# The first expert's tokens in two passes, its first weights from another queue: a delta-rule layer followed by a hash-routed mixture of experts

## The chip, the cores and the metric

The kernel runs on one core of a Trainium2 chip. The metric is the device time of one execution in microseconds (us). The kernel before takes 504.96 us (median of 3 runs, 503.61 to 505.69).

## The reference, cut to what matters

The first stage is a recurrence over 768 positions for 4 batches of 8 heads with 48 columns each. Its answers `y` become 3072 rows of 384 columns. The second stage sends each row to one of 8 experts, which a hash of the row's token picks, and writes the expert's answer to the row's place.

```python
k_n = k / (np.linalg.norm(k, axis=-1, keepdims=True) + 1e-06)
for t in range(S):                                   # S = 768
    kt, vt, bt = (k_n[:, :, t], v[:, :, t], beta[:, :, t, None])
    y[:, :, t] = np.einsum('bhd,bhde->bhe', q[:, :, t], state)
    v_old = np.einsum('bhde,bhd->bhe', state, kt)
    state = state + bt[:, :, :, None] * np.einsum('bhd,bhe->bhde', kt, vt - v_old)
x = y.transpose(0, 2, 1, 3).reshape(B * S, H * D)    # 3072 x 384
expert_idx = token_ids * np.int64(2654435761) % np.int64(E)   # E = 8
for e in range(E):
    mask = expert_idx == e
    h = np.maximum(x[mask] @ w1[e], 0.0)             # 384 x 1024
    out[mask] = h @ w2[e]                            # 1024 x 384
```

All data are float32. In these inputs the largest expert has 423 rows, of which 300 come from the first 17 chunks and 320 from the first 18.

## The kernel before, in words

**The recurrence** is worked in 24 chunks of 32 positions (`chunk`, c = 0 to 23). Four chunks are a group (g = 0 to 5). For each group `inverse` builds a triangular inverse on VectorE, column by column (L554, L558, L562), from the products of the keys `GK`, turns it into `TU` (L576), and `spread_t` lays it out as `Tz`: the group's first chunk by VectorE (L490), the other three by four DMAs of GpSimd (L497). A chunk is a chain between TensorE and ScalarE: ask the state for the keys (L593), scale by `Tz` (L632, `pair<-R,Tz`), copy to `W` (L651), update the state in PSUM (L661), copy the state back to SBUF (L716 on ScalarE; in the last chunks one half on VectorE, L714). The answers go through L632 and L686 to `x_sb`, and `store` scatters the chunk's rows to the DRAM tensor `x_scratch` in the order of the experts (GpSimd, L691). The rows of an expert therefore lie together, the earliest chunks first. `scale_v` (L504) prepares the values of the next chunk.

**What sets the order.** Each piece of work of this stage is a `task` with an engine, a duration and what it reads and writes. `order` lists them for all engines by a cost model, `boost` and `shy` (a task is held back that long). Each engine then works its own list strictly in that order, and an instruction that waits holds up all behind it on its engine. GpSimd's DMAs share eight semaphores in turn, so that a DMA can also wait for the eighth one before it.

**The first weights.** When the last inverse is done, its memory is free. There `load_w_parts` puts the first expert's `w1` (3 parts of 512 KB) and `w2` (4 parts of 384 KB), issued on SyncE behind the next stores.

**The experts** follow in falling order of their row counts, with fixed widths of 424, 424, 392, 392, 380, 380, 366 and 366 columns. `fetch` reads an expert's rows from `x_scratch` (four DMAs, L1084; those of the first expert from SyncE and ScalarE), `turn` transposes them on VectorE to `xT` (L1097), `gemm1` makes h (8 blocks of 3 products, each matmul of float32 being two instructions: 48 in all, L1115), which ScalarE and VectorE clear of negative values in turn (L1118, L1120) from three PSUM banks, and `turned` makes the answers (3 blocks of 8 products, 48 instructions, L1145), whose weights are every third column of `w2`. VectorE transposes them back (L1147), and GpSimd scatters them to the output (L1152). The last expert takes another path (L1128). The weights of expert e + 2 are loaded while expert e runs. Rows beyond the widths go through a loop at the end (L1197), which these inputs do not need.

Of the kernel before, what the change touches and what calls it, by code (L numbers as in the profile page):

```python
# [20 lines left out]
def kernel(  # L21
# [32 lines left out]
    NOV = (N - CAP + P - 1) // P  # L54
# [30 lines left out]
    def load_w_parts(e, pool):  # L85
        w1_sb = pool.tile([P, CO, F], F32, name="w1_sb")
        w2_sb = pool.tile([P, FO, DIN], F32, name="w2_sb")
        w1 = moe_w1[bass.ds(e, 1)].rearrange("o d f -> (o d) f")
        w2 = moe_w2[bass.ds(e, 1)].rearrange("o f d -> (o f) d")
        parts = [lambda i=i: nc.sync.dma_start(  # L90
            out=w1_sb[:, i], in_=w1.rearrange("(p co) f -> p co f", p=P)[:, i])
                 for i in range(CO)]
        parts += [lambda i=i: nc.sync.dma_start(
            out=w2_sb[:, i:i + 2],
            in_=w2[i * P:(i + 2) * P].rearrange("(o p) d -> p o d", p=P)) for i in range(0, FO, 2)]
        return (w1_sb, w2_sb), parts
# [15 lines left out]
    with ExitStack() as phase1:  # L112
# [34 lines left out]
        GKs = tiles(3, "GK", [P, C, GC, HU, 2])  # L147
# [360 lines left out]
        def inverse(g):  # L508
# [4 lines left out]
            def dve(ns, reads, writes, emit):  # L513
# [4 lines left out]
                U, zero[:, :, None].to_broadcast([P, C, C]), ACT.Copy), shy=24000 if g == 1 else 0, boost=-6e4 if g == 1 else 0)  # L518
# [9 lines left out]
                root, ssq, ACT.Sqrt, scale=0.25), boost=5e4)  # L528
# [51 lines left out]
        last_iv, stores = [0], set()  # L580
# [21 lines left out]
        def chunk(c):  # L602
# [96 lines left out]
            stores.add(len(tasks))  # L699
# [26 lines left out]
        def routing():  # L726
# [79 lines left out]
            own = new([P, 3, E])  # L806
            r_start, r_id, r_cnt = own[:, 0], own[:, 1], own[:, 2]
# [10 lines left out]
            for to, of in ((r_start, start), (r_id, iota_f[:, 0:E]), (r_cnt, cnt)):  # L818
# [4 lines left out]
                 lambda: nc.vector.tensor_copy(own_i, own[:, 0:2]))  # L823

            def tail():
                places, caps, room = new([P, NB_MAX]), new([P, E]), new([P, E])
                for e in range(E):
                    if e == 0 or WIDTHS[e] != WIDTHS[e - 1]:
                        dv("memset", caps[:, e:], float(WIDTHS[e]), **on)
                dv("tensor_scalar", out=places, in0=iota_f[:, 0:NB_MAX], scalar1=float(TB),  # L830
                   scalar2=low_f[:, 0:1], op0=ALU.mult, op1=ALU.add, **on)
                dv("tensor_tensor", room, r_cnt, caps, op=ALU.min, **on)
# [9 lines left out]
                thr, many = new([P, E, NOV]), new([P, E, NOV])  # L842
                dv("scalar_tensor_tensor", out=thr, in0=iota_f[:, None, 0:NOV].to_broadcast(
                    [P, E, NOV]), scalar=float(P), in1=caps[:, :, None].to_broadcast([P, E, NOV]),
                   op0=ALU.mult, op1=ALU.add, **on)
                dv("tensor_tensor", many, r_cnt[:, :, None].to_broadcast([P, E, NOV]), thr,
# [49 lines left out]
        def note():  # L896
# [93 lines left out]
            for c in range(NU):  # L990
# [7 lines left out]
                if c % GC == 2 and c + 2 < NU:  # L998
                    spread_t((c + 2) // GC)
# [256 lines left out]
```

## Time and profile before

| | us |
|---|---|
| median of 3 runs | 504.96 |
| the profiled execution | 505.14 |
| its span, first to last instruction | 503.5 |
| TensorE (PE) busy | 443.9 |
| VectorE (DVE) busy | 246.8 |
| ScalarE (ACT) busy | 165.4 |
| GpSimd (POOL) busy | 168.1 |

The span is what the trace covers; 1.64 us of the execution lie around it. The recurrence takes the first 228 us. The experts take the rest, and from 244 us to 494 us TensorE has no gap. A transfer is listed by the engine that issued it (SPq is SyncE's queue).

### The profile page before, as it was taken

Reading aid. Unit: us, or ns where it says so; the run is one execution under the profiler, and the core shown is the slowest. Engines: PE = TensorE matmul, PEld = TensorE weight load, DVE = VectorE, ACT = ScalarE, POOL = GpSimd, SP = SyncE. Lnnn points to the kernel's source line nnn. Section 1 sums busy time; section 2 is a strip of 40 time slices with the busy share of each in tenths; the row PEclk is TensorE's granted clock in tenths of the full one; section 3 lists DMA queues with packets and bytes.
Section 4 is the critical chain, followed back from the end, with each engine's and each line's share of the span. In section 5 each row is a group of like instructions: output and inputs, shape, how many; then the busy total and the mean of one; then the engine's idle time right before and its main releaser. Section 6 shows DMA issues by size and latency. Waiting matters only on the chain. (4 is left out here: it accounts for less than half of the span.)

```text
span 503.5 us, 15633 instructions
## 1 busy us (share of the span) xinstructions
PE 443.9 (88%) x6448; PEld 328.9 (65%) x6448; DVE 246.8 (49%) x882; ACT 165.4 (33%) x349; POOL 168.1 (33%) x224
## 2 busy tenths in 40 slices
PE   7796998879879697690999999999999999999993
PEld 4674877768768686580466566576676767767651
DVE  7799899999999989720212121121212212212100
ACT  4588778767676546440000100101001010010100
POOL 9752123132232312311000731715417063260721
PEclk8788799999989869976899999999999999999998
DMA  7965455466572622916973706409054190000000
GB/s 139 151 134 116 97 108 111 103 116 119 109 122 60 114 66 57 270 62 120 316 261 65 274 17 175 167 15 313 27 168 173 24 306 19 13 33 0 35 25 30
DMA packets 98248, 58.26 MB, mean 116 GB/s; under 512 B 84118, under 2 KB 92769, under 8 KB 97280
## 3 DMA queue, kind: packets, MB, share of 16 engines
q1 hardware_dynamic: 88832, 42.47, 34.3%
q0 software_dynamic: 7136, 14.12, 10.0%
q10 hardware_dynamic: 2208, 0.67, 0.8%
q8 instruction: 51, 0.84, 0.7%
q14 instruction: 21, 0.17, 0.1%
HBM read 44.51 MB, written 10.65 MB: 110 GB/s over the span
## 5 line engine op out<-in xcount | busy, mean ns | idle before, releaser
L1152 POOL DMA_INDIRECT out_dram<-o_sb,idx x90 | 88.3, 981 | 159.1 <-DVE o_sb L1147 133.8
L1115 PE MATMUL h_ps<-xT,w_sb 128*128 128x424 f32 (+3 forms) x384 | 129.2, 497 | 11.8 <-DMA xr<-x_scratch 11.8
L1115 PEld LDWEIGHTS h_ps<-xT,w_sb 128*128 128x128 f32 x384 | 73.8, 192 | 65.2 <-issue 27.9
L1145 PE MATMUL o_ps<-h_sb,w_sb 128*128 128x424 f32 (+3 forms) x336 | 112.3, 494 | 0.0
L1145 PEld LDWEIGHTS o_ps<-h_sb,w_sb 128*128 128x128 f32 x336 | 84.4, 251 | 27.1 <-issue 0.3
L1118 ACT ACTIVATE h_sb<-h_ps 128x424 f32<-128x424 f32 (+3 forms) x32 | 15.9, 496 | 233.2 <-PE h_ps L1115 233.2
L1120 DVE TENSOR_SCALAR h_sb<-h_ps 128x424 f32<-128x424 f32 (+3 forms) x32 | 18.1, 565 | 108.2 <-PE h_ps L1115 108.2
L691 POOL DMA_INDIRECT x_scratch<-x_sb,slot x24 | 25.3, 1052 | 115.5 <-ACT MT L480 45.4
L562 DVE TENSOR_TENSOR U<-U,tmp 128x30 f32<-128x30 f32 (+9 forms) x180 | 57.8, 321 | 0.0
L558 DVE TENSOR_TENSOR tmp<-U,Ni 128x30 f32<-128x30 f32 (+9 forms) x180 | 57.6, 320 | 0.1
L1147 DVE STREAM_TRANSPOSE o_sb<-o_ps 128x384 f32<-128x384 f32 (+2 forms) x21 | 15.5, 740 | 84.2 <-PE o_ps L1145 84.2
L593 PE MATMUL bank<-S,KQ 128*32 128x96 f32 x1472 | 40.4, 265 | 9.1 <-ACT S L716 6.1
L593 PEld LDWEIGHTS bank<-S,KQ 128*32 128x32 f32 x1472 | 34.3, 118 | 13.7 <-ACT S L716 8.0
L554 DVE SCALAR_TENSOR_TENSOR U<-U,Ni 128x1 f32<-128x1 f32 (+30 forms) x186 | 42.1, 226 | 0.2
L716 ACT ACTIVATE S<-psS 48x768 f32<-48x768 f32 x43 | 34.6, 805 | 18.0 <-PE psS L661 14.8
L661 PE MATMUL psS<-W,K 32*112 32x96 f32 x736 | 28.4, 285 | 7.6 <-ACT W L651 3.9
L632 PE MATMUL bank<-W,MT 64*64 64x48 f32 x768 | 31.0, 234 | 2.0 <-issue 1.5
L661 PEld LDWEIGHTS psS<-W,K 32*112 32x112 f32 x736 | 23.6, 188 | 10.9 <-ACT W L651 5.1
L632 PEld LDWEIGHTS bank<-W,MT 64*64 64x64 f32 x768 | 27.5, 148 | 4.9 <-issue 2.4
L497 POOL DMA_DIRECT2D Tz<-TU x24 | 17.5, 738 | 31.1 <-ACT S L901 14.5
L326 POOL DMA_DIRECT2D Q<-in_q_dram x40 | 23.0, 583 | 4.0 <-PE early L361 3.6
L480 ACT ACTIVATE MT<-GQ,kmask 128x256 f32<-128x256 f32 x48 | 21.8, 504 | 0.4 <-DVE GQ L442 0.4
(141 smaller groups left out, 441.3 us busy)
## 6 DMA issues: line engine op xcount, KB each, us to landing
w_sb<-in_moe_w_dram SPq DMA_DIRECT2D x14, 1536.0 KB, 9.9
V<-in_v_dram SPq DMA_DIRECT2D x96, 48.0 KB, 2.7
K<-in_k_dram SPq DMA_DIRECT2D x89, 48.0 KB, 3.1
Q<-in_q_dram SPq DMA_DIRECT2D x56, 48.0 KB, 3.1
xr<-x_scratch SPq DMA_DIRECT2D x16, 145.5 KB, 3.3
Tz<-TU POOLq DMA_DIRECT2D x24, 96.0 KB, 4.1
Q<-in_q_dram POOLq DMA_DIRECT2D x40, 48.0 KB, 3.7
w_sb<-in_moe_w_dram SPq DMA_DIRECT2D x3, 512.0 KB
```

The source lines that it names most:

```text
L326: eng].dma_start(out=dst[quarter(b)],
L554: nc.vector.scalar_tensor_tensor(out=U[:, n, 0:n], in0=U[:, j, 0:n], scalar=Ni[:, j, n:n + 1], in1=U[:, n, 0:n], op0=ALU.mult, op1=ALU.add)
L558: nc.vector.tensor_tensor(t, U[:, j:n, 0:n].to_broadcast([P, m, n]), Ni[:, j, n + 1:, None].to_broadcast([P, m, n]), op=ALU.mult)
L562: nc.vector.tensor_tensor(U[:, n + 1:, 0:n], U[:, n + 1:, 0:n], t, op=ALU.add)
L593: nc.tensor.matmul(res[quarter(b), u], lhsT=KQ[:, u, a, quarter(b)], rhs=S0[:, b, u].rearrange("p r d -> p (r d)"), start=(a == 1 and u == ...
L632: nc.tensor.matmul(to[rows, h], lhsT=lhsT(rows, h), rhs=rhs[rows, h], start=(first and h == 0), stop=True, skip_group_check=True, tile_pos ...
L661: nc.tensor.matmul(late["S"][0:DP + D, b, 2 * D * u:2 * D * u + 2 * D], lhsT=K4[quarter(b), u].rearrange("p r d -> p (r d)")[:, 0:DP + D], ...
L691: put = nc.gpsimd.indirect_dma_start(out=x_dram[:, :], out_offset=bass.IndirectOffsetOnAxis(ap=slot[:, c:c + 1], axis=0), in_=x_sb.rearran ...
L716: put = nc.scalar.activation(S1[half(r), :, :, r], new[half(r), :, :, r], ACT.Copy)
L1115: nc.tensor.matmul(h_ps[:, :width], lhsT=w1_sb[:, co, fo * P:(fo + 1) * P], rhs=xT[:, co, :width], start=(co == 0), stop=(co == CO - 1))
L1145: nc.tensor.matmul(os_ps[i][:, 0:width], lhsT=w2_sb[:, fo, i::CO], rhs=h_sb[:, fo, 0:width], start=(fo == 0), stop=(fo == FO - 1))
L1152: scat = nc.gpsimd.indirect_dma_start(out=out_q, out_offset=bass.IndirectOffsetOnAxis(ap=idx[e][:, k:k + 1], axis=0), in_=o_sb[:, k], in_o ...
```

## The change

1. **Two passes for the first expert.** As soon as the stores of the first 18 chunks are in DRAM, SyncE fetches the expert's first 288 rows (`fetch_first`) into the memory of `TU0`, and VectorE transposes them to `first["xT"]`. Behind the last chunk TensorE runs both products for these 288 columns, and then again for the other 136. The store of chunk 18 waits for that fetch.
2. **The first weights** are issued in seven parts by GpSimd, behind the stores of chunks 13, 14, 18, 19, 20, 21 and 21. `w1_first` takes the memory in which the key products `GK` lie, so that its parts can come before the last inverse is done. GpSimd loads the expert's number into a register for it. The fifth expert uses the same memory again.
3. **Bookkeeping.** The tables for overflowing rows get a ninth entry, for the case that the 288 rows are not all there in time; with these inputs they are, and the loop at the end stays empty.
4. **Order.** The clearing of `U` for a new inverse is held back by 8000 ns in all groups behind the first two and loses its rank, and the square root of the last inverse is held back by 1500 ns. VectorE's values for a chunk come a little earlier among the steps of the inverse.
5. `fetch(1)` and `weights(1)` stand ahead of the first pass, and the PSUM banks of the two products change places.

```diff
+    EARLY, ECH = 288, 18
+    EB = EARLY // TB
+    LATE = WIDTHS[0] - EARLY
+    w1_first = ctx.enter_context(tc.tile_pool(name="wk", bufs=1, side="right")).tile(
+        [P, CO, F], F32, name="w1_first")
...
-        GKs = tiles(3, "GK", [P, C, GC, HU, 2])
+        GKs = [w1_first[:, i].rearrange("p (j c u r) -> p j c u r", c=GC, u=HU, r=2)
+               for i in range(3)]
...
             task("ACT", 951, (), (f"U{i}",), lambda: nc.scalar.activation(
-                U, zero[:, :, None].to_broadcast([P, C, C]), ACT.Copy), shy=24000 if g == 1 else 0, boost=-6e4 if g == 1 else 0)
+                U, zero[:, :, None].to_broadcast([P, C, C]), ACT.Copy), shy=24000 if g == 1 else 8000 if g else 0, boost=-6e4 if g else 0)
...
-                root, ssq, ACT.Sqrt, scale=0.25), boost=5e4)
+                root, ssq, ACT.Sqrt, scale=0.25), boost=5e4, shy=1500 if g == NG - 1 else 0)
...
-            task("POOL", 1150, (f"x{c % 2}", "slot", "number"), (f"x_dram{c}",), store, kb=200)
+            task("POOL", 1150, (f"x{c % 2}", "slot", "number") + (("first_x",) if c >= ECH else ()),
+                 (f"x_dram{c}",), store, kb=200)
+
+        def fetch_first():
+            first["x"] = TUs[0].rearrange("p x i -> p (x i)")[:, 0:EB * QW].rearrange(
+                "p (k y) -> p k y", y=QW)
+            rows = x_dram[bass.ds(regs[0][0], EARLY)].rearrange(
+                "(k t) (q y) -> q t k y", t=TB, q=QN)
+            for qt in range(QN):
+                nc.sync.dma_start(out=first["x"][TB * qt:TB * qt + TB, :, 0:DQ + 1],
+                                  in_=rows[qt][:, :, 0:DQ + 1])
+
+        def first_parts(c):
+            for n, at in enumerate(PARTS):
+                if at == c:
+                    names = ([f"GK{n}{cc}{r}" for cc in range(GC) for r in range(2)]
+                             if n < CO else [f"w2{n}"])
+                    reads = (f"x_dram{c}", "e0") + (() if n < CO else (f"TU{(NG - 1) % 2}",))
+                    task("POOL", 900, reads, names, lambda n=n: w_parts(regs[3], first.get(
+                        "w2"))[n](nc.gpsimd), kb=512 if n < CO else 384)
+
+        PARTS = (13, 14, 18, 19, 20, 21, 21)
...
-                    w_tiles[0], parts = load_w_parts(regs[1][0], w_pool)
-                if i in stores and parts:
-                    for part in parts[:3]:
-                        part()
-                    parts = parts[3:]
+                    first["w2"] = w_pool.tile([P, FO, DIN], F32, name="w2_first")
+                    first["h"] = w_pool.tile([P, FO, EARLY], F32, name="h_first")
+                    first["xT"] = w_pool.tile([P, CO, EARLY], F32, name="xT_first")
...
             fetch(0, [(nc.sync, regs[0][0]), (nc.scalar, regs[2])])
             for t in os_ps:
                 nc.vector.memset(t[:, min(WIDTHS):], 0.0)
+            fetch(1)
+            weights(1)
+            w1_sb, w2_sb = w_tiles[0]
+            gemm1(w1_sb, first["xT"], first["h"], EARLY)
+            o_sb = m_o.tile([P, NB_MAX, DQ], F32, name="o_sb")
+            for i in range(CO):
+                turned(w2_sb, first["h"], o_sb, i, EARLY, 0)
+            scatter(idx_first, o_sb, range(EB))
...
-                gemm1(w1_sb, xTs.pop(e), h_sb, WIDTHS[e], between)
+                width = WIDTHS[e] if e else LATE
+                gemm1(w1_sb, xTs.pop(e), h_sb, width, between)
```

**Where instructions move.** On ScalarE, at chunk 15, the square root of the last inverse (`root`) stood ahead of both copies of the state, before:

```order
L623 ACTIVATE R_103<-bank_158 128x192 x2
L651 ACTIVATE W_105<-pair 128x192 x2
L527 ACTIVATE root_153<-ssq_151 128x32
L716 ACTIVATE S_96<-psS 48x16x48 x2
L686 ACTIVATE x_sb_107<-bank_159 128x4x96
```

and now:

```order
L632 ACTIVATE R_111<-bank_163 128x192 x2
L660 ACTIVATE W_113<-pair 128x192 x2
L748 ACTIVATE S_104<-psS 48x16x48
L536 ACTIVATE root_158<-ssq_156 128x32
L748 ACTIVATE S_104<-psS 48x16x48
L695 ACTIVATE x_sb_115<-bank_164 128x4x96
```

It moved behind the first of the two copies; the second still stands behind it.

On GpSimd, chunks 17 to 19 before (`x_scratch<-x_sb` is a chunk's store, `Tz` the layout of the last inverse for chunks 21 to 23):

```order
L690 COPY x_sb_107<-number 128x4
L691 DMA x_scratch<-x_sb_107,slot 3520x400
L690 COPY x_sb_106<-number 128x4
L691 DMA x_scratch<-x_sb_106,slot 3520x400
L497 DMA Tz_135<-TU_137 32x24x32 x4
L690 COPY x_sb_107<-number 128x4
L691 DMA x_scratch<-x_sb_107,slot 3520x400
```

and now:

```order
L699 COPY x_sb_115<-number 128x4
L700 DMA x_scratch<-x_sb_115,slot 3520x400
L699 COPY x_sb_114<-number 128x4
L700 DMA x_scratch<-x_sb_114,slot 3520x400
L506 DMA Tz_140<-TU_142 32x24x32 x4
L699 COPY x_sb_115<-number 128x4
L700 DMA x_scratch<-x_sb_115,slot 3520x400
L99 ISA
L99 DMA w_first<-in_moe_w_dram 128x1024
```

Stores and layout keep their order. The second store shown, that of chunk 18, now waits for the early fetch, and the layout stands behind it; a part of the weights follows the store of chunk 19.

On ScalarE, at the end of the recurrence, before:

```order
L686 ACTIVATE x_sb_107<-bank_159 128x4x96
L1084 ISA
L1084 DMA xr<-x_scratch 32x14x97
L1084 ISA
L1084 DMA xr<-x_scratch 32x14x97
L1169 TENSOR_LOAD ov_i
L1118 ACTIVATE h_sb<-h_ps_4900 128x424
```

and now:

```order
L695 ACTIVATE x_sb_115<-bank_164 128x4x96
L1147 ISA
L1147 DMA xr<-x_scratch 32x5x97
L1147 ISA
L1147 DMA xr<-x_scratch 32x5x97
L1183 ACTIVATE h_first<-h_ps_4939 128x288
L1183 ACTIVATE h_first<-h_ps_4941 128x288
```

ScalarE's two fetches of the remaining rows, which wait for the last store, still stand first; its share of the first pass stands behind them.

## Rows read from the trace of the kernel before

**Rows 1.** Windows of 40 us: length, busy time (and count) by engine, granted clock, DMA.

```profile
160.00:200.00 40.00, 32.57 (x960) 29.03 (x949) 36.88 (x147) 22.37 (x52) 10.24 (x15) 0.83 0.36 78
```

**Rows 2.** Timeline, end of the recurrence: start, length, what, idle before it and releaser.

```profile
227.15 1.14 PE L632 MATMUL bank<-W,MT 64*64 64x48 f32 x32 [0.49 <-ACT W L651]
228.39 0.49 ACT L686 ACTIVATE x_sb<-bank 128x384 f32<-128x384 f32 x1 [1.06 <-issue]
229.65 0.98 POOL L691 DMA_INDIRECT x_scratch<-x_sb,slot  x1 [3.12 <-issue]
232.65 3.55 SPq L1084 DMA_DIRECT2D xr<-x_scratch  x6
232.92 1.22 ACTq L1084 DMA_DIRECT2D xr<-x_scratch  x2
239.07 2.10 DVE L1097 STREAM_TRANSPOSE xT<-xr 128x448 f32<-128x448 f32 x3 [6.43 <-DMA xr<-x_scratch]
240.06 19.25 PE L1115 MATMUL h_ps<-xT,w_sb 128*128 128x424 f32 x48 [11.77 <-DMA xr<-x_scratch]
```

**Rows 3.** Timeline of TensorE alone, three stretches of equal matmuls, start and length.

```profile
276.22 6.21 PE L1115 MATMUL h_ps<-xT,w_sb 128*128 128x424 f32 x17
...
451.77 10.62 PE L1145 MATMUL o_ps<-h_sb,w_sb 128*128 128x366 f32 x34
...
101.62 0.60 PE L361 MATMUL pair<-ident,Q 128*128 128x128 f32 x4
```

**Rows 4.** Groups by line, TensorE's weight loads: count, busy us, mean ns, idle before.

```profile
L1145 PEld LDWEIGHTS o_ps<-h_sb,w_sb 128*128 128x128 f32 x336 | 84.4, 251 | 27.1 <-issue 0.3
L1115 PEld LDWEIGHTS h_ps<-xT,w_sb 128*128 128x128 f32 x384 | 73.8, 192 | 65.2 <-issue 27.9 <-DVE xT L1097 0.4 <-DVE o_sb L1147 0.2
L593 PEld LDWEIGHTS bank<-S,KQ 128*32 128x32 f32 x1472 | 34.3, 118 | 13.7 <-ACT S L716 8.0 <-issue 4.8 <-ACT x_sb L686 0.6
```

**Rows 5.** Timeline around two waits of ScalarE, chunks 6 and 15.

```profile
108.79 1.06 ACT L517 ACTIVATE U<-zero 128x1024 f32<-128x1024 f32 x1 [2.43 <-DVE TU L576]
...
171.72 0.23 ACT L527 ACTIVATE root<-ssq 128x32 f32<-128x32 f32 x1 [2.92 <-DVE ssq L524]
...
173.52 2.79 PE L593 MATMUL bank<-S,KQ 128*32 128x96 f32 x64 [2.78 <-ACT S L716]
```

**Rows 6.** Windows of 4 us, columns as in rows 1.

```profile
172.00:176.00 4.00, 2.48 (x64) 2.44 (x64) 3.86 (x21) 3.28 (x7) 1.41 (x4) 0.53 0.73 124
...
212.00:216.00 4.00, 3.52 (x78) 3.23 (x76) 0.74 (x1) 1.24 (x3) 0.19 (x1) 0.65 0.89 324
242.00:246.00 4.00, 4.00 (x10) 1.96 (x9) 0.00 (x0) 0.53 (x1) 0.00 (x0) 0.76 0.95 388
```

**Rows 7.** Timeline, chunks 17 to 21.

```profile
184.48 0.57 DVE L504 TENSOR_TENSOR bank<-V,ntok 128x384 f32<-128x384 f32 x1 [1.84 <-ACT R L623]
...
191.15 0.98 POOL L691 DMA_INDIRECT x_scratch<-x_sb,slot  x1 [6.07 <-ACT MT L480]
...
197.98 1.95 DVE L576 STREAM_TRANSPOSE TU<-U 128x1024 f32<-128x1024 f32 x1
...
200.55 2.94 POOL L497 DMA_DIRECT2D Tz<-TU  x4 [2.40 <-PE psS L661]
...
203.45 1.13 PE L632 MATMUL pair<-R,Tz 64*64 64x48 f32 x32
...
211.15 0.57 PE L593 MATMUL bank<-S,KQ 128*32 128x96 f32 x17 [2.67 <-issue]
...
211.66 1.24 PE L632 MATMUL pair<-R,Tz 64*64 64x48 f32 x32
```

**Rows 8.** DMA issues: whole run, then 180 to 235 us; KB each, median us to landing.

```profile
Tz<-TU POOLq DMA_DIRECT2D x24, 96.0 KB, 4.1
...
w_sb<-in_moe_w_dram SPq DMA_DIRECT2D x4, 384.0 KB, 12.2
Tz<-TU POOLq DMA_DIRECT2D x4, 96.0 KB, 7.5
```

More of the change, by code (lines that the diff above doesn't have):

```diff
@@ L578, in inverse @@
             last_iv[0] = len(tasks) - 1
-        last_iv, stores = [0], set()
+        last_iv, first = [0], {}
         def pairs(us):
@@ L697, in store, with turn_first @@
                 tc.add_to_no_dep_group("rows", put.ins)
-            stores.add(len(tasks))
-            task("POOL", 1150, (f"x{c % 2}", "slot", "number"), (f"x_dram{c}",), store, kb=200)
+            task("POOL", 1150, (f"x{c % 2}", "slot", "number") + (("first_x",) if c >= ECH else ()),
[8 more added lines that the diff above has]
+                                  in_=rows[qt][:, :, 0:DQ + 1])
+        def turn_first(i):
+            nc.vector.transpose(
+                first["xT"][:, i].rearrange("p (k t) -> p k t", t=TB), first["x"][:, :, i:DQ:CO])
+        def first_parts(c):
[7 more added lines that the diff above has]
+        PARTS = (13, 14, 18, 19, 20, 21, 21)
         to_load = {w: iter(range(AHEAD + 1, NU)) for w in "kq"}
@@ L999, in note, with first_e @@
                     spread_t((c + 2) // GC)
+                first_parts(c)
+                if c == ECH - 1:
+                    task("SP", 2000, tuple(f"x_dram{n}" for n in range(ECH)) + ("regs",),
+                         ("first_x", "TU0"), fetch_first, kb=450)
+                    for i in range(CO):
+                        task("DVE", 370, ("first_x", f"TU{(NG - 1) % 2}"), (f"xT{i}",),
+                             lambda i=i: turn_first(i))
                 if c == NU // 2:
                     registers_later[0]()
+                    def first_e():
+                        regs[3] = nc.values_load(own_i[0:1, 1, 0:1], min_val=0, max_val=E - 1,
+                                                 engines=[mybir.EngineType.Pool])
+                    task("POOL", 900, ("own", f"R{c % 2}0"), ("e0",), first_e)
                 if c == NU - 2:
@@ L1037 @@
             seq, start = order()
-            parts = []
             for i in seq:
@@ L1146, in turned, with scatter @@
                                  rhs=h_sb[:, fo, 0:width], start=(fo == 0), stop=(fo == FO - 1))
[L1147 removed]
+            nc.vector.transpose(o_sb[:, k0:k0 + n, i::CO],
                                 os_ps[i][:, 0:n * TB].rearrange("p (k t) -> p k t", t=TB))
[L1150 to L1151 removed]
+        def scatter(of, o_sb, blocks):
+            for k in blocks:
                 scat = nc.gpsimd.indirect_dma_start(
[L1153 to L1154 removed]
+                    out=out_q, out_offset=bass.IndirectOffsetOnAxis(ap=of[:, k:k + 1], axis=0),
                     in_=o_sb[:, k], in_offset=None, bounds_check=QN * N - 1, oob_is_err=False)
@@ L1172 @@
             places(0)
-            fetch(1)
-            weights(1)
             for e in range(E):
-                w1_sb, w2_sb = w_tiles.pop(e)
+                w1_sb, w2_sb = w_tiles[e]
                 def between(fo):
@@ L1190 @@
                             places(e + 1)
-                        turned(e, w2_sb, h_sb, o_sb, i)
-                    scatter(e, o_sb)
+                        turned(w2_sb, h_sb, o_sb, i, width, skip)
+                    scatter(idx[e], o_sb, range(skip, NBS[e]))
                 else:
```

120 lines of the change are left out of this document (74 added, 46 removed).

## Prediction

> **What bounds the kernel now.** I read the windows first, then the timeline around the end of the recurrence, then the waits of TensorE there, then TensorE's weight loads and the DMA issues. Two places matter.
>
> *The seam.* The last answers leave TensorE at 227.15 + 1.14 = 228.29. From there a single chain runs: answers to SBUF, the store at 229.65, its landing (SyncE can issue the fetch at 232.65, 3.0 later), the fetch and its flight, VectorE's transposes at 239.07, the first product at 240.06, with TensorE idle for 11.77 [rows 2]. The product then takes 19.25 for 48 instructions, because the granted clock is 0.76 in 242:246 and lower before [rows 2, 6]. Expert 1 begins at 276.22 [rows 3]. So the first expert occupies 276.22 − 228.29 = 47.93 us behind the recurrence. From 244 to 494 TensorE has no gap, so what starts earlier here ends earlier: the 227.3 us of rest of the span do not change.
>
> *The last inverse.* In 160:200 VectorE is busy for 36.88 of 40 [rows 1], with the inverse's columns; `TU` is ready at 197.98 + 1.95 = 199.93, and chunk 20 scales with it at 203.45. GpSimd issues the layout for the later chunks at 200.55, over 2.94, and chunk 21 scales only at 211.66 [rows 7]. Of these 8.2 us 2.67 are TensorE idle with "issue" as its reason [rows 7]; without them a chunk takes 5.5. At that time the first expert's weights are in flight: the layout's four DMAs land in 7.5, against 4.1 over the whole run, and the `w2` parts in 12.2 [rows 8]. I read the issue wait as instructions that came late through the same crowd; the trace shows only that both stand together.
>
> **How long a narrow pass takes.** Three stretches of equal matmuls fit one line, 0.84 ns a column plus 0.16 for the last one's drain: 17 × 424 columns give 6.05 + 0.16 = 6.21 (6.21 in the trace), 34 × 366 give 10.45 + 0.16 = 10.61 (10.62), 4 × 128 give 0.43 + 0.16 = 0.59 (0.60) [rows 3]. Nothing is added per instruction, though each has a weight load of its own: the loads lie beside the matmuls. So 288 columns are 0.242 each, 11.6 for 48. For 136 columns the matmul is 0.114, shorter than the mean load: 0.192 for the first product, 0.251 for the second, whose weights are every third column [rows 4]. A listed load may contain waiting, since 32 columns are listed with 0.118 [rows 4], and that is no quarter of 0.192. Lower ends for the 136 columns are 48 × 0.114 = 5.5 for each product; upper ends are 48 × 0.192 = 9.2 and 48 × 0.251 = 12.05. For contiguous weights I take 5.5, because the transposes with 128 contiguous columns and a load each do run at 0.11 [rows 3]. For strided ones no row is near; I take 0.17 (the listed 0.251 less the 0.08 that a load seems to have whatever its width, an estimate from 0.118 and 0.192), 8.2.
>
> The Trainium skill speaks against this change: "TensorE: Matmul & The Clock Gate", Part 3, says that a weight load overlaps running matmuls only when it targets other rows of the array, while Part 2 there also allows a load into a background buffer. By the first, a full-height load would add to every matmul; by the second it is hidden. The trace agrees with the second (0.84 ns a column at three widths, no constant). It stays a rival below.
>
> **Part 1, the two passes (term A).** The first pass waits for the last answers only; its fetch, transposes and weights are long done. Its chain:
> - start behind the last matmul: 0.1.
> - first product, 288 columns: 11.6, and in it a stall. ScalarE's own list has the two fetches of the late rows ahead of its evictions. They wait for the last store, and are issued up to 232.92 + 1.22 = 234.14 [rows 2]. TensorE can fill three PSUM banks, 18 matmuls or 4.35 us, to 232.7; the fourth block needs ScalarE's first eviction, done near 234.6. Stall 1.9. Bounds: 0, if the DMA issues don't hold ScalarE up, to 3.9, if the clock then falls and costs 2.0 as it did now (19.25 against 48 × 0.356 + 0.16 = 17.25).
> - second product, 288 columns: 11.6 (12.05 by the strided loads).
> - between the passes VectorE must transpose the last answers and then the late rows: 2.10 for 3 × 448 columns [rows 2] is 0.70 for one, hence 0.45 + 3 × 0.25 + 0.1 for semaphores = 1.3. The rows themselves have landed long before (239 against about 253). Bounds 0.5 to 2.
> - 136 columns: 5.5 and 8.2.
>
> Sum: 0.1 + 11.6 + 1.9 + 11.6 + 1.3 + 5.5 + 8.2 = 40.2, against 47.93: **A = −7.7**. With loads at full length 48.2, +0.3 (+2.3 with the clock's loss); with no stall and all loads hidden 35.6, −12.3.
>
> **Parts 2 and 4, the recurrence's end (term B).**
> - `root` waited 2.92 for VectorE and so kept back the state's copies: TensorE idled 2.78 at 173.52, and was granted 0.53 in 172:176, nearly all at 1.2 GHz [rows 5, 6]. VectorE in turn idled 1.84 at 184.48 for ScalarE [rows 7]. One copy now stands ahead of `root`, the other still behind, so half of the chain's delay may stay. Since VectorE sets when `TU` comes, only its gap counts: I take 1.5, bounds 0 and 3.1 (all that rows 1 leave idle).
> - The clearing of `U` waited 2.43 at 108.79 [rows 5]; that is early, and what it delayed was caught up before the inverse. Zero, bound −1.
> - The weights go out over chunks 13 to 21 and no longer in one burst. Layout at its usual 4.1: it is there 0.62 + 2.94 + 4.1 = 7.7 behind `TU`, not 11.7. Chunk 21 then follows chunk 20 by 5.5, and the 2.67 go (0 if the three last parts still crowd). Of 212:216, granted 0.65 [rows 6], some 70% ran at 1.2 GHz, which cost 1.4; I count them as gone, since the idle time before them is.
> - The parts cost GpSimd some 1 us each (0.7 for an issue, by 2.94 for four), beside 10.24 busy of 40 [rows 1]: hidden. What they could hide no more is late stores, which nobody waits for until the end.
> - The store of chunk 18 waits for the early fetch, and the layout stands behind it on GpSimd. Chunk 17's store at 191.15 [rows 7] + 3.0 landing + 6.4 (232.65 to 239.07 [rows 2]) = 200.55, when the layout is issued now: 0, since `TU` would be only 1.5 earlier. Bound: the fetch takes 12.2 as `w2` did, the layout goes out at 207.3, chunk 21 scales at 207.3 + 2.94 + 4.1 = 214.4, 2.7 later than now.
> - VectorE gets three transposes of 288 columns, 0.45 each, among the last chunks; two may delay a state copy: +0.9 (0 to 1.4).
>
> Sum: −1.5 − 2.67 − 1.4 + 0.9 = **B = −4.7**, bounds +3.6 and −8.6.
>
> **Parts 3 and 5** move a few loads and register reads to engines that wait: zero, ±0.5. 320 of the expert's rows come from 18 chunks, so all 288 are there and the loop stays empty.
>
> Total: 505.14 − 7.7 − 4.7 = 492.7. The profiled execution is 0.2 above the median, so **492.5 us**; its own range 488 to 497.
>
> **Rivals.**
> 1. *Weight loads set the pace of the 136 columns* with their full length (0.192, 0.251). For it: they are listed so [rows 4]. Against: 0.11 for transposes [rows 3]. A is +0.3: 505 without B, 500 with it. Chance 0.13.
> 2. *The recurrence gains in full, and strided loads are hidden*: `TU` 3.1 earlier, 2.67, both stretches of low clock gone (2.8), no cost on VectorE, second product 5.5: 505 − 8.6 − 7.7 − 2.7 = 486. For it: each loss has one cause in the rows. Against: VectorE has hardly a gap to give [rows 1]. Chance 0.17.
> 3. *The early fetch holds GpSimd*, so the layout comes later: B = +2.7, and 505.1 − 7.7 + 2.7 = 500. For it: both use one queue [rows 7]. Against: the crowd is gone. Chance 0.07.
> 4. *Slower: loads are not hidden in narrow passes but add.* The place is both products of 136 columns, 48 × (0.192 + 0.114) + 48 × (0.251 + 0.114) = 32.2 instead of 13.7, and A becomes +10.8: 516 without B, 511 with it. It decides from 0.08 us added per instruction (7.7 / 96). Against: no constant in rows 3. Chance 0.05.
>
> The forecast has 0.58. A run of this kernel can tell 0.5%, 2.5 us, from no change. Faster: forecast, rival 2, rival 3 and half of rival 1, 0.88; same 0.07; slower 0.05. The range, 484.5 to 501, leaves out rival 4, the bad half of rival 1 and a tail of rival 2.
>
> **What would show it.** Right: TensorE's first product directly behind the last answers; a wait for ScalarE at its fourth block; 136-column matmuls 0.114 apart in the first product and 0.15 to 0.2 in the second; layout landing in some 4 us; chunk 21 scaling 5 to 6 behind chunk 20; expert 1 at about 264. Wrong: spacing near 0.19 and 0.25 (rival 1) or 0.3 (rival 4); layout issued far behind `TU` (rival 3); clock still near 0.5 around chunks 15 and 21, or an end of the recurrence at 228 as now, which takes B away and leaves 497.

## The result, and the profile after

The changed kernel takes 499.62 us (median of 20 runs, 493.5 to 504.6), the kernel before 505.05 in 20 runs beside them (500.87 to 509.47). The ratio is 0.988, with a 95% interval of 0.985 to 0.991: faster by some 6 us, a little under half of the 12.5 forecast. The ratio leaves out executions more than 1.5% above the fastest of their kernel, seven of the changed kernel's 20, the traced one among them, and so comes out lower than the medians' 0.989. The time lies in the range, the size of the gain was missed.

The traced execution took 502.01 us, 2.4 above its median, with a span of 500.4. TensorE's timeline at the seam (start, length, what, idle before it and its releaser), which answers to [rows 2, 3]:

```profile
224.79 0.92 PE L641 MATMUL bank<-W,MT 64*64 64x48 f32 x25
226.35 4.63 PE L1180 MATMUL h_ps<-xT_first,w_first 128*128 128x288 f32 x18 [0.64 <-ACT x_sb L695]
231.72 7.54 PE L1180 MATMUL h_ps<-xT_first,w_first 128*128 128x288 f32 x30 [0.74 <-ACT h_first L1183]
239.10 11.80 PE L1210 MATMUL o_ps<-h_first,w_first 128*128 128x288 f32 x48
252.25 5.18 PE L1180 MATMUL h_ps<-xT,w_first 128*128 128x136 f32 x42 [1.34 <-issue]
258.48 0.96 PE L1180 MATMUL h_ps<-xT,w_first 128*128 128x136 f32 x6 [1.05 <-issue]
259.28 2.24 PE L1210 MATMUL o_ps<-h_sb,w_first 128*128 128x136 f32 x12
263.47 0.62 PE L1210 MATMUL o_ps<-h_sb,w_first 128*128 128x136 f32 x2 [1.95 <-issue]
264.97 6.95 PE L1210 MATMUL o_ps<-h_sb,w_first 128*128 128x136 f32 x34 [0.88 <-DVE h_sb L1185]
...
271.75 17.24 PE L1180 MATMUL h_ps<-xT,w_sb 128*128 128x424 f32 x48
```

The first pass is much as forecast: it starts 0.64 behind the last answers (0.1 forecast), waits 0.74 for ScalarE at its fourth block (1.9 forecast), and ends at 250.9; the gap to the second pass, the bubble below, is 1.35. Then the second pass takes 271.75 − 252.25 = 19.5 us where 13.7 were forecast. The first product's instructions are listed 0.12 apart, as forecast, but stop at the eighth block, and the second product's stop later for `h_sb`. The first expert comes to 46.0 us, against 47.93 before.

The other engines in the second pass. ScalarE and VectorE clear a block by turns as soon as it is complete (an eviction below), and so free its PSUM bank:

```profile
251.79 1.02 POOL L1217 DMA_INDIRECT out_dram<-o_sb,idx_first  x1 [23.64 <-DVE last_i L1243]
...
255.38 0.30 DVE L1185 TENSOR_SCALAR h_sb<-h_ps 128x136 f32<-128x136 f32 x1 [1.02 <-PE h_ps L1180]
...
258.14 0.28 ACT L1183 ACTIVATE h_sb<-h_ps 128x136 f32<-128x136 f32 x1 [3.18 <-issue]
...
260.30 0.30 DVE L1185 TENSOR_SCALAR h_sb<-h_ps 128x136 f32<-128x136 f32 x1 [4.63 <-PE h_ps L1180]
...
262.10 0.98 POOL L1217 DMA_INDIRECT out_dram<-o_sb,idx_first  x1 [0.30 <-issue]
...
263.13 0.28 ACT L1183 ACTIVATE h_sb<-h_ps 128x136 f32<-128x136 f32 x1 [4.71 <-remote]
...
264.62 0.30 DVE L1185 TENSOR_SCALAR h_sb<-h_ps 128x136 f32<-128x136 f32 x1 [4.01 <-PE o_ps L1210]
```

Four blocks are cleared 0.2 us behind their last matmul; the fifth to eighth come 2.3, 3.7, 5.9 and 5.3 us behind it (worked out from the starts and the spacing). Over the same stretch GpSimd runs the nine scatters of the first pass's answers, 1.28 us apart.

The last product ends 10.1 us before the span does (500.4 − 490.31):

```profile
474.67 15.64 PE L1193 MATMUL o_ps<-w_sb,h_sb 128*122 128x384 f32 x48
```

In the trace before it was 8.7 us (503.5 − 494.78):

```profile
479.14 15.64 PE L1128 MATMUL o_ps<-w_sb,h_sb 128*122 128x384 f32 x48
```

The prediction had nothing for this end.

### The profile page after: what moved, and what is told of

It is laid out like the page before. It is cut to its first block, busy times and chain, and to the rows that moved or that the text cites. A ratio compares the mean times of both kernels' runs of the same rounds, so it can differ in the third digit from the quotient of the medians.

```text
span 500.4 us, 15902 instructions
## 1 busy us (share of the span) xinstructions
PE 448.2 (90%) x6544; PEld 341.6 (68%) x6544; DVE 251.8 (50%) x903; ACT 165.2 (33%) x353; POOL 174.5 (35%) x231
## 5 line engine op out<-in xcount | busy, mean ns | idle before, releaser
L1217 POOL DMA_INDIRECT out_dram<-o_sb,idx x81 | 79.3, 979 | 133.0 <-DVE o_sb L1212 110.4
L1180 PE MATMUL h_ps<-xT,w_sb 128*128 128x392 f32 (+3 forms) x288 | 94.5, 488 | 0.0
L1183 ACT ACTIVATE h_sb<-h_ps 128x392 f32<-128x392 f32 (+4 forms) x32 | 14.9, 466 | 220.3 <-PE h_ps L1180 198.9
L1180 PEld LDWEIGHTS h_ps<-xT,w_sb 128*128 128x128 f32 x288 | 54.7, 190 | 38.2 <-issue 7.8
L1210 PE MATMUL o_ps<-h_sb,w_sb 128*128 128x392 f32 (+3 forms) x240 | 79.6, 491 | 0.0
L1210 PEld LDWEIGHTS o_ps<-h_sb,w_sb 128*128 128x128 f32 x240 | 60.3, 251 | 18.8 <-issue 0.2
L1185 DVE TENSOR_SCALAR h_sb<-h_ps 128x392 f32<-128x392 f32 (+4 forms) x32 | 16.9, 527 | 104.7 <-PE h_ps L1180 63.7
L1212 DVE STREAM_TRANSPOSE o_sb<-o_ps 128x384 f32<-128x384 f32 (+4 forms) x24 | 16.1, 671 | 84.2 <-PE o_ps L1210 84.2
L602 PEld LDWEIGHTS bank<-S,KQ 128*32 128x32 f32 x1472 | 34.0, 117 | 13.5 <-ACT S L748 7.4
L748 ACT ACTIVATE S<-psS 48x768 f32<-48x768 f32 x43 | 34.6, 806 | 19.7 <-PE psS L670 17.2
L1210 PE MATMUL o_ps<-h_sb,w_first 128*128 128x136 f32 (+1 forms) x96 | 25.3, 426 | 2.8 <-issue 1.9
L506 POOL DMA_DIRECT2D Tz<-TU x24 | 17.5, 738 | 24.1 <-ACT Tz L949 12.2
L1210 PEld LDWEIGHTS o_ps<-h_sb,w_first 128*128 128x128 f32 x96 | 21.4, 267 | 6.5 <-issue 2.1
```

The lines of the kernel that those rows point to most:

```text
L506: lambda b=b, x0=x0: nc.gpsimd.dma_start(out=Tz[quarter(b), x0:, b % 2], in_=TU[quarter(b), x0:]), kb=150)
L602: nc.tensor.matmul(res[quarter(b), u], lhsT=KQ[:, u, a, quarter(b)], rhs=S0[:, b, u].rearrange("p r d -> p (r d)"), start=(a == 1 and u == ...
L748: put = nc.scalar.activation(S1[half(r), :, :, r], new[half(r), :, :, r], ACT.Copy)
L1180: nc.tensor.matmul(h_ps[:, :width], lhsT=w1_sb[:, co, fo * P:(fo + 1) * P], rhs=xT[:, co, :width], start=(co == 0), stop=(co == CO - 1))
L1210: nc.tensor.matmul(os_ps[i][:, 0:width], lhsT=w2_sb[:, fo, i::CO], rhs=h_sb[:, fo, 0:width], start=(fo == 0), stop=(fo == FO - 1))
L1217: scat = nc.gpsimd.indirect_dma_start(out=out_q, out_offset=bass.IndirectOffsetOnAxis(ap=of[:, k:k + 1], axis=0), in_=o_sb[:, k], in_offse ...
```

## The experiments

Three pieces are read from each trace. B is the end of the recurrence, counted from the moment at which the first inverse's `TU` is ready, since the start-up before it varies by 4 us between executions. "First expert" runs from the last answers to expert 1. "End" is what follows the last product. The median is of all executions, the pieces are of one traced execution, which can lie up to 3.3 us beside it (`wait_sp` 496.27, `burst` 493.7). Three runs of one execution each (`noscat`, `four`, `drop`) stand in the text alone. `contig` takes other weights for 136 rows, `drop` leaves 288 rows unwritten.

| run, chip | median us | ratio to before | B | first expert (second pass) | end |
|---|---|---|---|---|---|
| before, first trace | 505.05 | | 182.3 | 47.9 | 8.7 |
| before2, 3 | 505.24 | | 181.4 | 49.2 | 8.7 |
| changed, first trace | 499.62 | 0.988 [0.985, 0.991] | 179.4 | 46.0 (19.5) | 10.1 |
| again, 7 | 499.54 | 0.990 [0.985, 0.995] | 177.4 | 46.1 (19.5) | 10.4 |
| early, 7 | 498.59 | 0.988 [0.983, 0.993] | 177.2 | 46.1 (19.5) | 10.0 |
| late, 7 | 501.06 | 0.993 [0.989, 0.997] | 178.8 | 46.1 (19.5) | 10.1 |
| contig, 7 | 498.9 | 0.985 [0.977, 0.993] | 179.7 | 45.3 (18.8) | 10.2 |
| even, 7 | 492.45 | 0.975 [0.970, 0.981] | 176.3 | 39.6 (17.1) | 10.1 |
| again2, 3 | 499.54 | 0.988 [0.984, 0.993] | 176.6 | 46.2 (19.7) | 10.2 |
| wait2, 3 | 491.67 | 0.973 [0.970, 0.976] | 177.8 | 40.6 (14.1) | 10.1 |
| even2, 3 | 494.02 | 0.976 [0.972, 0.980] | 178.6 | 39.6 (17.2) | 10.1 |
| wait, 5 | 489.08 | 0.973 [0.968, 0.978] | 173.4 | 41.3 (14.1) | 10.3 |
| burst, 5 | 490.88 | 0.976 [0.971, 0.982] | 175.6 | 41.0 (14.1) | 10.1 |
| order4, 5 | 492.37 | 0.980 [0.975, 0.986] | 175.4 | 40.8 (14.1) | 10.4 |
| again3, 1 | 490.72 | 0.976 [0.970, 0.983] | 174.7 | 41.3 (14.1) | 10.0 |
| wait_even, 1 | 489.39 | 0.972 [0.969, 0.976] | 176.4 | 39.0 (16.6) | 10.3 |
| wait_sp, 1 | 493.0 | 0.979 [0.975, 0.983] | 180.1 | 41.0 (14.1) | 9.3 |

**again.** No edit.

> The changed kernel once more, for a second trace. In its first trace the pieces of the sum came out as: end of the recurrence 2.6 us earlier (4.7 forecast), first expert 1.9 shorter (7.7 forecast), of which the second pass alone is 19.5 instead of 13.7. If these are features of the kernel, this trace shows the second pass at 19 to 20 again, with evictions that come 2 to 6 us behind their matmuls from its fifth block on. If they were an accident of one execution, the second pass takes 14 to 16 here.

The second pass took 19.5 us again, with evictions up to 4.6 us late. It is no accident of one execution. The recurrence ended 2.4 us earlier than in the first trace.

**early, late.** The third expert's weights are moved away from the second pass:

```diff
             weights(1)
+            weights(2)                 # early
...
-                        weights(e + 2)
+                        if e:
+                            weights(e + 2)
```

```diff
-                        weights(e + 2)
+                        for n in () if e == 0 else (2, 3) if e == 1 else (e + 2,):
+                            weights(n)     # late
```

> The third expert's weights (3 MB) are issued behind the second's, before the first pass, and so are in long before the second pass. Theory 1 (crowd: while the DMA engines are full, the signals between TensorE and the evicting engines come late, and narrow blocks have no slack for it): no late eviction in the second pass, 48 x 0.12 + 48 x 0.20 = 15.5 us instead of 19.5, time 4 us below the changed kernel, 495.5. Theory 2 (TensorE itself falls behind in narrow matmuls, since their weight loads take 0.19 to 0.25): second pass stays at 19 to 20, time within 1 us of the changed kernel. Theory 3 (GpSimd's nine scatters disturb): as theory 2.

> The third expert's weights are issued one expert later, behind the rows of the fourth. Theory 1 (crowd): second pass at 15 to 16 us instead of 19.5, time 4 us below the changed kernel, the same as with the early issue. Theory 2 (weight loads) and theory 3 (scatters): second pass stays at 19 to 20. If the late rows' small packets alone make the crowd, the second pass lies between, 17 to 18.

Both 19.5, with evictions as late as before, in `early` from the sixth block on with the DMA engines busy for a fifth of the time or less (254 to 260 us; for the fifth they were full). Theory 1, the crowd, falls for these blocks.

**contig.** Neighbouring columns of `w2` for the second product of the second pass:

```diff
-                nc.tensor.matmul(os_ps[i][:, 0:width], lhsT=w2_sb[:, fo, i::CO],
+                nc.tensor.matmul(os_ps[i][:, 0:width], lhsT=w2_sb[:, fo, i * P:(i + 1) * P] if k0 else w2_sb[:, fo, i::CO],
```

> In the second pass alone the second product takes its weights from 128 neighbouring columns of w2 instead of every third (so the answers of those 136 rows are not the reference's). If the strided load sets the spacing of 0.20 us there, the 34 unhindered matmuls come at 0.114 to 0.12 each, and the pass is some 4 us shorter in its unhindered part. If reading the rows or the clock sets it, it stays at 0.20. If the late signals alone rule the pass (theory 1), its end moves by less than 2 us.

The instructions now came 0.12 apart (median of the listed starts; 0.176 in `again`), so the stride does set that spacing. The pass shortened by only 0.75 us, and its last 34 instructions, behind the halts, took 6.26 us in place of 6.98. The clock explains the rest. Columns as in rows 1, first `contig`, then `again`:

```profile
261.00:267.00 6.00, 3.98 (x17) 3.98 (x18) 2.01 (x4) 0.00 (x0) 0.97 (x3) 0.50 0.82 305
...
261.00:267.00 6.00, 4.46 (x21) 4.47 (x22) 2.28 (x5) 0.00 (x0) 0.44 (x2) 0.72 0.69 256
```

At the lower clock (1.2 GHz) the instructions come 0.227 apart in both, so that the stride costs nothing there.

**four.** Every accumulation of the second pass four times:

```diff
-                for co in range(CO):
+                for co in list(range(CO)) * times:
...
-            for fo in range(FO):
+            for fo in list(range(FO)) * (4 if k0 else 1):
...
+                gemm1(w1_sb, xTs.pop(e), h_sb, width, between, 1 if e else 4)
```

> In the second pass every accumulation is run four times over into the same bank (results unchanged): 192 instructions of 136 columns in each product in place of 48. It measures the sustained spacing by itself. Theory 2, weight loads set it: 0.19 an instruction in the first product, so 27 us more there, 0.20 to 0.25 in the second, 29 to 36 more. If narrow matmuls are sustained at their listed spacing and only something at the pass's start is late: 0.116, 17 us more in the first, and 0.12 to 0.18 (17 to 26) in the second.

TensorE's timeline in that pass:

```profile
251.54 7.95 PE L1180 MATMUL h_ps<-xT,w_first 128*128 128x136 f32 x66 [1.35 <-issue]
...
262.54 0.51 PE L1180 MATMUL h_ps<-xT,w_first 128*128 128x136 f32 x3 [0.71 <-issue]
...
263.99 13.47 PE L1180 MATMUL h_ps<-xT,w_first 128*128 128x136 f32 x114 [0.43 <-issue]
277.30 22.90 PE L1210 MATMUL o_ps<-h_sb,w_first 128*128 128x136 f32 x131
```

The run took 540.66 us. 114 instructions of 136 columns run at 13.47 / 114 = 0.118 us, each with its own load of 128 columns; 131 with strided loads at 22.90 / 131 = 0.175. TensorE halts only between about 8 and 12 us behind the pass's start, in steps, with "issue" as the reason and inside a block of 24 instructions (66 is no multiple of it), so for no eviction; the second block's eviction comes 6.8 us late. Theory 2, that weight loads hold TensorE at 0.19 and more, falls. The Trainium skill says in "TensorE: Matmul & The Clock Gate", Part 3, that a weight load overlaps running matmuls only when it goes to other rows of the array. That does not show here either: 0.118 is 136 × 0.84 ns plus 0.004.

**noscat.** The scatters moved down GpSimd's list, behind the second pass:

```diff
-            scatter(idx_first, o_sb, range(EB))
...
+                    if e == 0:
+                        scatter(idx_first, o_sb, range(EB))
```

> The nine scatters of the first pass's answers are issued behind the second pass instead of beside it. Late evictions did not go away without the crowd of the weights (in the runs with earlier and later weights the second pass stayed at 19.5 us). Theory 3 (the scatters disturb): second pass 15 to 16 us here, no late evictions. Theory 2 (TensorE itself sustains no more in narrow matmuls, and the listed starts run ahead of it): 19.5 again.

It took 502.32 us, the second pass 19.7. Nothing was tested: nothing ahead of the scatters on GpSimd waits, so they went out at the same time as ever. A place in an engine's list delays nothing unless something ahead of it waits.

**even.**

```diff
-    EARLY, ECH = 288, 18
+    EARLY, ECH = 224, 18
```

> 224 early columns and 200 late ones instead of 288 and 136. Theory 2 (no matmul below 0.19 to 0.2 us, whatever its width): first pass 96 x 0.19 to 0.2 + 0.7, second 96 x 0.2, with the bubble of 1.5 some 40 to 41 us in place of 46.1, so 5 us less time than the changed kernel: 494. If width alone counted (0.84 ns a column) and a disturbance in the second pass adds 5.8 us to it: 18.8 + 1.5 + 16.1 + 5.8 = 42, 4 less. If nothing but the sum of the columns counts, 46, no change.

First expert 39.6 us. The evictions of the second pass are late here too, but by 3.3 us at most; they hold TensorE for 0.3 us at its eighth block, and the last of them starts 9.7 us behind the start of the pass. With seven scatters instead of nine that is 2.6 us sooner than in `again` (12.4), two scatters of 1.28. That pointed at GpSimd.

**drop, wait, burst, order4** ran together on chip 5.

```diff
-            scatter(idx_first, o_sb, range(EB))       # drop: only this
...
+                    if e == 0:                         # wait: these too
+                        nc.vector.tensor_copy(idx_late, idx_first)
+                        scatter(idx_late, o_sb, range(EB))
```

```diff
-        PARTS = (13, 14, 18, 19, 20, 21, 21)
+        PARTS = (19,) * 7                              # burst
```

```diff
-   ... shy=24000 if g == 1 else 8000 if g else 0, boost=-6e4 if g else 0)
+   ... shy=24000 if g == 1 else 0, boost=-6e4 if g == 1 else 0)      # order4
-                root, ssq, ACT.Sqrt, scale=0.25), boost=5e4, shy=1500 if g == NG - 1 else 0)
+                root, ssq, ACT.Sqrt, scale=0.25), boost=5e4)
```

> The nine scatters of the first pass's answers are left out (288 rows of the output stay unwritten). In the run that only moved them down GpSimd's list they still went out beside the second pass, since nothing ahead of them waits, so that run told nothing of them. Theory 3 (GpSimd's scatters hold back TensorE's signals as long as they run, some 12.3 us from the start of the second pass with nine, 9.5 us with seven): signals in time, second pass 48 x 0.118 + 48 x 0.175 + 0.2 = 14.3 us instead of 19.5. Theory 2 (a narrow stream holds itself back in its first 12 us): 19.5 as before.

> The same nine scatters are made to wait for the second pass's last transpose (they take their row numbers from a copy that VectorE makes there). Theory 3: second pass 14.3 us, first expert 40.8 instead of 46.1, time 5 us below the changed kernel, unless the scatters, now beside the second expert's wide product, cost there. Theory 2: no change from the changed kernel.

> All seven parts of the first weights are issued at once behind the store of chunk 19, nearly as before the change, the rest as in the changed kernel. If spreading them is worth what was forecast (2.7 of waiting at chunk 21 and up to 1.4 of low clock), the recurrence ends 3 to 4 us later than with pieces, at 227 to 228 for a last inverse at 198, and the layout of the last inverse lands late, 7 us instead of 4. If the queue by which they go out matters and not the crowd, it ends as in the changed kernel, 24 to 26 us behind chunk 19's answers.

> The clearing of U and the square root of the last inverse get their former delays and ranks back, the rest as in the changed kernel. If these orders bring VectorE's last inverse forward by 1.5 us as forecast, it is ready at 199.5 to 200 here instead of 198.1 (mean of eight traces), chunk 15 to 16 takes 8 to 9 us instead of 6.4, and the kernel is 1.5 us slower. If they bring nothing, 198 again.

All four have a second pass of 14.1 (`drop` took 490.83 us), `burst` and `order4` with their scatters beside it. So these alone did not make the late evictions. `burst` told against the forecast on another point: the recurrence ended 22.9 us behind the last `TU`, near the other runs of that chip (23.1 to 23.6), and the layout landed in 4.1. Spreading the parts is not what helps. `order4` had the former waits back (TensorE idle for 2.52 behind `root`, the next chunk 7.2 us instead of 6.0; 9.0 from chunk 15 to 16, as expected), but from the first `TU` to the last took 151.9 us, against 150.3 to 152.7 in the three others: no gain for VectorE can be told from that spread.

**again2, before2, wait2, even2** on one chip, to tell chip from scatters; no new edits.

> The changed kernel itself, beside the kernel before and three others on one chip. Theory C (the chip decides): where the recurrence's chunks run at 6.0 us without a pause in TensorE, the second pass takes 14.1 us and the kernel 490 to 491; where they run at 6.4, 19.5 and 499. Theory S (the scatters decide everywhere): 19.5 us on either chip, with evictions up to 6 us late.

> The kernel before, for its trace on the same chip. Theory C: its chunks 16 to 19 run at 6.0 or 6.4 us apart as in the changed kernel on this chip, its wide products show no late eviction on either, so that it loses less than 3 us where the changed kernel loses 8. The end of the recurrence is at 227 to 229 if the former trace was typical.

> The first pass's scatters wait for the second pass. On a chip with the pause: second pass 14.1 if the scatters take part in it, 19.5 if not. On a chip without: 14.1, and no difference from the changed kernel beyond 1 us.

> 224 and 200 columns. Without the pause both passes go by 0.84 ns a column, and only the strided product of 136 columns (0.175 instead of 0.114, 2.9 us) has something to give: first expert 38.5 to 39.5 in place of 40.8, 1 to 2 us less time than the changed kernel. With the pause 39.6 in place of 46.1, 6.5 less.

**wait_sp, wait_even, again3** on one chip. `wait_even` is `wait` with 224 columns; `wait_sp` is `wait` with

```diff
-                    task("POOL", 900, reads, names, lambda n=n: w_parts(regs[3], first.get(
-                        "w2"))[n](nc.gpsimd), kb=512 if n < CO else 384)
+                    task("SP", 900, reads, names, lambda n=n: w_parts(regs[1][0], first.get(
+                        "w2"))[n](nc.sync), kb=512 if n < CO else 384)
```

> As the run with waiting scatters, but the seven parts of the first weights are issued by SyncE, behind the same stores. If GpSimd's seven extra DMAs make its drain at the end longer, the stretch from TensorE's last product to the end of the span falls from 10.4 to 8.9 us and the kernel gains 1.5. If the scatters in smaller portions or the program's length make it, it stays at 10.4. If issue by SyncE crowds out the layout of the last inverse, that lands in over 5 us instead of 4, and the recurrence ends over 2 us later.

> Waiting scatters and columns 224 and 200 together. The first pass 18.9 + 1.6 of stall, the bubble 1.5, the second 8.1 + 8.4: 38.9 in place of 40.8 with waiting scatters alone, so 1.5 to 2 us less time than that; if the second pass of 136 columns lost nothing to its strided loads, no difference.

> The changed kernel on the same chip as these two. If its chunks 16 to 19 are 6.0 us apart here, theory C gives a second pass of 14.1 and 490 to 491 us; if 6.4, one of 19.5 and 499.

TensorE in `again2` (chip 3), the changed kernel, one chunk of the recurrence and the second pass:

```profile
188.04 0.90 PE L641 MATMUL pair<-R,Tz 64*64 64x48 f32 x22
189.09 0.53 PE L641 MATMUL pair<-R,Tz 64*64 64x48 f32 x10 [0.16 <-issue]
...
250.22 5.18 PE L1180 MATMUL h_ps<-xT,w_first 128*128 128x136 f32 x42 [1.34 <-issue]
257.27 0.96 PE L1180 MATMUL h_ps<-xT,w_first 128*128 128x136 f32 x6 [1.87 <-issue]
...
263.07 7.00 PE L1210 MATMUL o_ps<-h_sb,w_first 128*128 128x136 f32 x34 [0.86 <-DVE h_sb L1185]
```

In `wait2` on the same chip, the scatters waiting:

```profile
247.25 5.87 PE L1181 MATMUL h_ps<-xT,w_first 128*128 128x136 f32 x48 [1.34 <-issue]
252.95 8.54 PE L1211 MATMUL o_ps<-h_sb,w_first 128*128 128x136 f32 x48
```

In `again3` (chip 1), the changed kernel again, the same two places:

```profile
183.91 1.14 PE L641 MATMUL pair<-R,Tz 64*64 64x48 f32 x32
...
245.83 5.87 PE L1180 MATMUL h_ps<-xT,w_first 128*128 128x136 f32 x48 [1.34 <-issue]
251.53 8.54 PE L1210 MATMUL o_ps<-h_sb,w_first 128*128 128x136 f32 x48
```

On chips 3 and 7 TensorE pauses in most chunks, mostly while it scales by `Tz` (1.4 to 1.65 us where 1.14 is usual), and chunks 16 to 19 are some 6.4 us apart; on chips 1 and 5 there is hardly a pause (one such chunk in `wait_sp`), and they are 6.0 apart. The second pass is late only where the pause and the scatters come together: on chip 3 it loses 5.6 us with the scatters beside it and nothing without them, on chip 1 nothing even with them.

`before2`, the kernel before on chip 3, has late evictions too, against what was expected of it. The second expert's first product is listed from 276.05 on, with GpSimd's scatters beside it. VectorE clears the sixth and the eighth block; the line between them is TensorE's next product:

```profile
289.06 0.60 DVE L1120 TENSOR_SCALAR h_sb<-h_ps 128x424 f32<-128x424 f32 x1 [3.67 <-PE h_ps L1115]
...
293.13 7.28 PE L1145 MATMUL o_ps<-h_sb,w_sb 128*128 128x424 f32 x20
...
295.80 0.60 DVE L1120 TENSOR_SCALAR h_sb<-h_ps 128x424 f32<-128x424 f32 x1 [6.14 <-remote]
```

The eighth block is complete at 293.13 and cleared 2.7 us later. Five of the next six experts show it by 0.7 to 2.6 us; the first expert, without scatters beside it, does not, and neither does any wide product in the first trace of before or in `again3` (0.3 us at most). TensorE loses nothing by it here (20 × 0.356 + 0.16 = 7.28): the next product needs the eighth block only at its eighth step, at about 298. So the delay belongs to the scatters and the chip, and the change only made it cost something.

In the narrow pass the waits also let the clock fall: TensorE stood still before 263, and in `again2` it was granted half, 1.2 GHz, for the next stretch:

```profile
264.00:266.00 2.00, 2.00 (x11) 2.00 (x10) 0.81 (x2) 0.00 (x0) 0.00 (x0) 0.50 0.74 269
```

What the pause is stays open, and so does whether TensorE's signals are late or its work runs behind its listed starts; the halts inside a block in `four` speak for the second. The traces with the pause hold 7,700 to 8,000 semaphore updates, those without it 9,500 to 9,700, for nearly the same program, so the recording of events may have a part in it; every timed run was also recorded, so that time and trace cannot be told apart on this. The chips of the two first traces are not on record. The kernel before runs its chunks 6.0 us apart there from chunk 18 on and has 9,531 updates, so it counts with chips 1 and 5; the changed kernel has the pause.

`wait_sp` gave back what the weights' new queue had brought: 5.4 us of B in its trace, 2.3 us in the median (493.0 against 490.72 for `again3`; the traced execution was the longest of six). TensorE there, at chunks 20 and 21, and the window behind its idle time:

```profile
203.40 1.19 PE L603 MATMUL bank<-S,KQ 128*32 128x96 f32 x47
...
208.87 1.01 PE L603 MATMUL bank<-S,KQ 128*32 128x96 f32 x17 [4.28 <-issue]
```

```profile
209.00:216.00 7.00, 6.51 (x117) 5.81 (x119) 1.89 (x5) 1.35 (x3) 0.19 (x1) 0.50 0.01 2
```

This is the picture of [rows 6, 7], larger: 47 matmuls, 4.28 of "issue", 17 matmuls, then half clock. SyncE put its four `w2` parts out together as soon as the last `TU` was done (196.6), beside the layout:

```profile
196.73 2.94 SPq L103 DMA_DIRECT2D w_first<-in_moe_w_dram  x4
...
197.24 2.93 POOL L507 DMA_DIRECT2D Tz<-TU  x4 [2.31 <-PE bank L603]
```

Where GpSimd issues them behind the layout, even nearly all at once, the idle time is absent:

```profile
200.11 2.95 POOL L506 DMA_DIRECT2D Tz<-TU  x4 [2.35 <-PE bank L602]
...
206.44 1.68 POOL L99 DMA_DIRECT2D w_first<-in_moe_w_dram  x3
```

(GpSimd in `burst`.) From the last `TU` the recurrence needed 29.3 us in `wait_sp`, 28.4 and 28.7 in the two traces of before, 23.1 in `again3`, 22.9 in `burst`. Queue and moment changed together here, so this does not show which of them counts. What fills the "issue" is not shown either: in the gap of `wait_sp` the trace has a 16 KB packet of instructions under way from 206.00 to 207.43, but not for whom. The end was 9.3 with SyncE, 10.0 and 10.3 in the two beside it, 8.7 before. GpSimd's closing instruction (DRAIN) accounts for 0.9 of that: it takes 3.50 us in both traces of before and in `wait_sp`, 3.66 in `drop`, and 4.40 in every other trace, whatever the chip. The remaining 0.1 to 0.8 lies between the last product and this instruction and is open.

`wait_even` has the lowest ratio, 0.972 [0.969, 0.976] at 489.39 us, not to be told from 0.973 for `wait` (489.08 us, chip 5). Its first expert is 2.3 us shorter than the changed kernel's on its chip (39.0, 38.9 expected), its median 1.3 us lower. In `even2`, with the pause, the first expert is 6.6 us shorter and the median 5.5 lower. On chip 1 the change itself is worth 503.1 − 490.72 = 12.4 us.

## Why the prediction was wrong

**The step that failed: the 136 columns at 5.5 and 8.2, in the sum of term A.** On a chip without the pause they take 5.7 and 8.4. On the others they take 19.5 together, because the evictions come up to 6 us late while the first pass's scatters run beside these narrow products: with the scatters moved away the pass takes 14.1 on the same chip (`again2`, `wait2`). Most of the 5.6 are halts; half clock behind them makes up to 1 us (34 instructions in 7.00, at 0.175 they take 5.95). The prediction priced the waits inside the pass by matmuls and loads alone, and did not list the scatters among what lies beside it; nor did it count with a chip whose rows differ from those of its one trace. Term A came out at −1.9 in the first trace and −2.9 in `again2` against `before2`, where −7.7 was forecast; −6.6 in `again3` against the first trace of before. That last is 1.1 short: 0.5 for the wait from the last matmul to the first (0.63, forecast 0.1), 0.2 in the bubble, 0.4 in the narrow products. The stall of 1.9 was 0.74 of idle time where the first pass ran at full clock. In `again3` the first 5 us of the pass were granted 0.66, TensorE did not wait, and the product took 13.4: near the 13.5 forecast, but by luck.

**Rival 1 came near the number (500) by luck: its mechanism was not there.** Its 9.2 + 12.05 = 21.25 for the second pass are not far from the 19.5, but `four` shows 0.118 and 0.175 sustained. What would have parted them was written down: spacing near 0.19 and 0.25. The listed spacing was 0.12 and 0.175. That the product stood still between such stretches had no rival.

**Term B (−4.7) was of the right size, with its parts wrong.** From the first `TU` the changed kernel gained 2 to 5 us with the pause (against `before2`) and 7.6 without (`again3` against the first trace of before). The part from the last `TU` on gave 2.0 to 5.3 where 2.67 + 1.4 − 0.9 = 3.2 were forecast. The reason given, that pieces spread the load, fell with `burst`; what `burst` and `wait_sp` show is that it helps to issue the parts behind the layout, as GpSimd's queue does, and not beside it. The 1.5 of `TU` cannot be told from the spread. The early fetch did not hold the layout up (199.58 in the first trace, 0.6 behind `TU`): rival 3 was not seen.

So the 12.4 us on chip 1 are near the forecast by compensation: A fell 1.1 short, B gave 2.9 more, and the end cost 1.3.

**Costs put at nothing.** The end of the kernel takes 1.3 to 1.7 us longer, 0.9 of it in GpSimd's DRAIN. Parts 3 and 5 were not run by themselves, so their zero is not shown.

**Rival 2** had the strided loads hidden; they are not (0.175 against 0.118 in `contig`). **Rival 4** (loads add to matmuls) is excluded by `four`. The strided load at 0.17, an estimate from a mean and a supposed fixed share, measured 0.175; the two means give 0.09 for that share and not 0.08, hence 0.16. The bound for a late fetch has a slip too: 191.15 + 3.0 + 12.2 is 206.35, not 207.3, so that the layout would have made chunk 21 later by 1.7, not 2.7.

## What to carry to other kernels

When a change makes products narrower, list what else runs beside them, and not only what they wait for: a wide block hid a late eviction (2.7 us in `before2`) that a narrow one cannot. A burst of weights that must not delay a small transfer is issued behind it, most simply on the same queue; spreading it was not needed here. And a second trace of the kernel before, from another chip, shows which of its intervals belong to the program.

## What had not been expected of the hardware

- The same program shows 6.0 us a chunk on two chips and 6.4 on two others. The kernel before differs by 2 us between their medians (503.1 and 505.24), the changed kernel by 9 (490.72 and 499.54).
- TensorE's instructions can be listed at full pace while the engines that read its results see them up to 6 us later, on two of four chips and with scatters on GpSimd beside them.
- 128 × 128 float32 weights from every third column make 136-column matmuls 0.175 us apart, from neighbouring columns 0.118.
- GpSimd's DMAs lengthen its closing DRAIN, behind all work, by about 0.1 us each: 3.50 us without the seven parts of weights, 4.40 with them, 3.66 with the parts but without nine scatters.
